# Attention and a gated MLP on one core: the opening loads 288 keys and 512 queries first, and two pairs are turned by DMA

## The chip, the cores and the metric

The kernel runs on one core of one Trainium2 chip. Its time is the device time of one execution in microseconds (us); a lower time is better. A core has five engines with a queue of instructions each: TensorE (PE in the profile; matrix products and transposes), VectorE (DVE), ScalarE (ACT), GpSimd (POOL) and SyncE (SP, which here only issues DMAs). DMAs issued by SP and ACT go through hardware queues (q1 and q10 in the profile), those of GpSimd through a software queue (q0); all are carried out by the same sixteen DMA engines. An engine does its instructions in the order in which they stand in its queue, and an instruction that waits holds up all behind it.

## The reference

Attention for 8 batches of 8 heads (576 positions, head size 64) with a bias that depends on the distance of two positions, then a two-layer network with a periodic activation:

```python
scores = scale * np.matmul(q, k.transpose(0, 1, 3, 2))
bias = bias_table[bucket]                       # bucket of |i - j|
scores = scores + bias.transpose(2, 0, 1)[None, :, :, :]
attn = softmax(scores)
x = (attn @ v).transpose(0, 2, 1, 3).reshape(B * S, H * D)   # 4608 x 512
h = x @ w_in                                    # 512 -> 2048
s = np.sin(alpha * h)
g = h + s * s / (alpha + 1e-09)
out = g @ w_out                                 # 2048 -> 512
```

## The kernel before

Heads are worked on in pairs (64 + 64 rows of the 128 partitions), four pairs (0 to 3) to a batch. For a pair the keys and queries are brought into the form head-size x position (`kT`, `qT`). A **score unit** is one block of 128 keys against 512 queries of both heads of a pair: two matmuls into PSUM, one exponential on ScalarE that writes `u` in half precision, one multiplication on VectorE by the exponential of the bias (`m2r`). A pair has four such units ("A") and one for the last 64 keys ("C"), whose bias tile is `mhr`. Then TensorE forms u times v (AV), with a column of ones that gives the sum; VectorE divides (a reciprocal `rd` and a product, the normalization), and the result, positions x features, is turned into features x positions, `xT`. Products of `xT` with `w_in`, the activation and products with `w_out` follow. Attention of the next batch runs between these.

The first batch is special: nothing covers it. Its keys and queries are loaded in single precision (`natx` for pair 0, on SP's queue, `nat` for pairs 1 to 3, by GpSimd), converted, and transposed on TensorE (lines 594 and 600), 96 positions at a time, then copied out of PSUM (L583). Fillers (`zz`) keep TensorE running meanwhile. The bias table goes a way of its own: `tabN` and `phi_sb` are multiplied on TensorE, exponentiated on ScalarE (`tabE`), multiplied with `phi_sb` again, copied to `e_sb` (L649), written to DRAM in `e_dram` from ScalarE's queue (L650), and read back by SP in the shifted forms `m2r` (L516) and `mhr` (L523). GpSimd's copy `tick` (L675) waits for `m2r`, and the loads of `w_in` (L481) stand behind it. `clear` (L491 to L497) sets the padding of `kt`, `vh` and `v` once for each of two buffers. The normalizations of pairs 0 to 2 (L1056, L1057) give the tile `s`, which TensorE turns with four transposes each (L1088) and VectorE or ScalarE copies into `xT` (L583, L581). Later batches turn theirs with a DMA transpose from SP's queue (L1079, L970).

The order on each engine is made when the program is built: the class `Plan` holds tasks with a cost on each engine that may take them, a priority and for some a due time `nb`, and its `run` plays them through with these costs and writes each engine's instructions in the order that comes out. The constants in capitals (`T_...` due times in us, `..0` priorities of the first batch) set that order and nothing else: on the chip each instruction waits for its inputs, not for a due time. The units of the first batch come in this order:

```python
runs = ((a, "A", 0), (a, "A", 1), (a, "A", 2), (a, "C", 0), (a, "A", 3),
        (b, "A", 0), (b, "A", 1), (b, "C", 0), (b, "A", 2), (b, "A", 3))
```

for the pairs a, b = 0, 1 and then 2, 3.

Of the kernel before, what the change touches and what calls it, by code (L numbers as in the profile page):

```python
# [64 lines left out]
class Plan:  # L65
# [89 lines left out]

    def run(self, t0):
        free = {e: t0 for e in ("PE", "ACT", "DVE", "POOL", "SP")}
        todo = list(self.tasks)
        while todo:
            best = None  # L160
            cands = {e: [] for e in free}
            over = []
            look = 0
            for t in todo:
                look += 1
                if look > WINDOW:
                    break
                r = self.ready(t)
                if r is None:
                    continue  # L170
                for e in t.engs:
                    if e == "ACT" and t.s_only and not self.sin:
                        continue
                    st = max(free[e], r)
                    if t.fill and self.in_qk and self.used >= OFFSET + self.quota * self.share:
                        over.append((st, t))
                        continue
                    cands[e].append((st, t))
            if over and min((x[0] for x in cands["PE"]), default=1e9) > free["PE"] + FILL_GAP * min(
                    x[1].part for x in over):  # L180
                cands["PE"] += over
            for e, c in cands.items():
                if not c:
                    continue
                s0 = min(x[0] for x in c)
                st, t = min(((x[0], x[1]) for x in c if x[0] <= s0 + SLACK[e]),
                            key=lambda x: (x[1].pri, x[0]))
                fin = st + t.engs[e]
                if best is None or (st, fin) < best[:2]:
                    best = (st, fin, e, t)  # L190
            if best is None:
                raise RuntimeError("nothing can go on")
            st, fin, e, t = best
            if e == "PE" and WARM_FROM < free[e] < WARM_END and st > free[e] + WARM_GAP:
                if self.fill(free[e], 192):
# [29 lines left out]
WARM_END = 22.0  # L225
QUOTA = 47
QUOTA1 = 28
OFFSET = 0
T_START = 4.0
STEPS = {0: ((1, 1, 1, 1),) * 3, 1: ((3, 1),) * 3}  # L230
T_W0 = 24.5
PRI_S = 0
T_WI = 16.8
T_TAB = 5.2
T_CL = 24.5
T_FIRST = (4.75, 5.95)
T_PAIR = ((7.9, 8.5), (9.3, 10.2), (11.6, 12.3))
T_ACT = ()
T_M2 = (14.6, 15.4, 16.6, 17.2)
T_MH = 15.4  # L240
T_RST = 25.0
T_V0 = (5.8, 6.4, 8.9, 9.6)
T_P3 = 7.0
T_VA = (10.5, 11.0)
T_VB = 19.5
V_AT = {1: (4, 5, 6, 7)}
V_PRI = -1000
T_AL = (10.0, 560)
LATE = 100
P_ST = 3  # L250
WIDE = 3
T_TP = ((150, 150), (650, 650), (1500, 1500))
GA = 0.0
GB = 0.0
GUARD = {"A": GA, "B": GB, "C": 0.0, "X": 0.0}
T_LD = 33.0

AV_AT = (3, 4, 6, 7)
AV_D = (0, 0, 300, 0)
# [7 lines left out]
MIX = "nnssss"  # L267
SUMS = {1: (0, 1, 2, 3)}
PACE = ((0, 0), (0, 0), (2, 1), (8, 1))
T_WS = (43.0, 48.3, 48.3, 48.3)  # L270
# [9 lines left out]
T_V = ((15.5, 19.0), (50.0, 50.0))  # L280
T_TR1 = ((32.0, 33.5), (35.0, 36.5))
T_W = (25.5, 30.5)
T_WO = (40.5, 43.0, 45.7, 48.3)
WARM0 = 8
WARM1 = 2
WARM_LAG = 0.3
WARM_GAP = 0.12
WARM_FROM = 7.3
AV_PRI = 0
NORM_PRI = 200  # L290
CP_PRI = 0
# [16 lines left out]
def kernel(  # L308
# [39 lines left out]
    for x in range(EW - 1):  # L348
# [39 lines left out]


    natx = tp.tile([128, NF * DM], F16, name="natx", tag="g", bufs=2)  # L390
    N0 = 2 * 2 * SI * D
    nat0 = natx[0:SN, 0 : 2 * N0].bitcast(F32).rearrange("s (kq h x) -> s kq h x", kq=2, h=2)
    natb = natx[0:SN, 2 * N0 : 3 * N0].rearrange(
        "s (kq i two d) -> s kq i two d", kq=2, i=SI, two=2
    )
# [65 lines left out]
    def load_v32(h):  # L461
        nc.sync.dma_start(out=vst[:, h], in_=v[0, h, 0:512].rearrange("(c p) d -> p c d", p=128))
# [10 lines left out]
    def load_nat(dst, h0, h1, src, eng):  # L473

        eng.dma_start(out=dst, in_=src[h0:h1].rearrange("h (p i) d -> p h (i d)", i=SI))
# [30 lines left out]
    def warm1(k, n):  # L506
        full(pb[:, k, 0:n], zz[:, 0:128], zz[:, 0:n], True, True)

    def cast0(kq, eng):
        eng.tensor_copy(  # L510
            out=natb[:, kq], in_=nat0[:, kq].rearrange("s two (i d) -> s i two d", i=SI)
        )

    def load_m2r(eng, h0, h1, r):

        eng.dma_start(  # L516
# [18 lines left out]
    load_nat(nat0[:, 0], 0, 2, k[0], nc.sync)  # L535
    load_nat(nat0[:, 1], 0, 2, q[0], nc.sync)
# [19 lines left out]
    cast0(0, nc.vector)  # L556
    x0 = nat0[:, 1].rearrange("s two (i d) -> s i two d", i=SI)
    nc.vector.tensor_copy(out=natb[:, 1, :, 0], in_=x0[:, :, 0])
    P_.tensor_copy(out=natb[:, 1, :, 1], in_=x0[:, :, 1])

    def loads2():
        for h in (0, H // 2):
# [22 lines left out]
    def plan_tr(t, p, kq, pri, nb, deps=()):  # L585
# [42 lines left out]

        return [x], [plan.add({"POOL": 0.4 if t == 0 else 0.5}, tail, [x], pri + 30)]

    def plan_table():

        a, b = Buf("h"), Buf("h")
# [12 lines left out]
            full(bank(b)[0:H, 0:EW], tabE, phi_sb, True, True)  # L646

        def cp(e):
            nc.scalar.activation(out=e_sb, in_=bank(b)[0:H, 0:EW], func=AF.Copy)  # L649
# [12 lines left out]
        plan.add({"ACT": 1.1}, cp, [x], -1100, use=[b])  # L662

    def plan_v0():
        plan.add({"POOL": 1.4}, lambda e: load_pair(3), [], 9001, nb=T_P3)
# [141 lines left out]
    def plan_att0(g, gates, gate):  # L807

        u, ub, done = Cell(), Buf("u"), {}
        a, b = 2 * g, 2 * g + 1  # L810
        runs = ((a, "A", 0), (a, "A", 1), (a, "A", 2), (a, "C", 0), (a, "A", 3),
                (b, "A", 0), (b, "A", 1), (b, "C", 0), (b, "A", 2), (b, "A", 3))
        exps, head = [], []
        for i, unit in enumerate(runs):
            base = PB + 3200 * g + 300 * i
            x = plan_unit(0, *unit, u, ub, done, gate, base)
            p, kind, _ = unit
            deps = gates + tr[(0, p, 0)][1 if kind == "C" else 0] + tr[(0, p, 1)][0]

            def run(e, i=i, x=x):  # L820
                if i == 0:
# [183 lines left out]
    def plan_av(t, parts, u, ub, done, base, dma):  # L1005
# [65 lines left out]
            rows = S * t + q0, S * t + parts[-1][1] + 128  # L1071
            xdone.append((t, rows, p0, x))

        if dma:

            def turn(e):
                o = (xT[:, p0 : p0 + 2, x0 : x0 + 128] if two else
                     xT[:, p0, x0 : x0 + 128 * nq].rearrange("d (c q) -> d c q", c=nq))
                nc.sync.dma_start_transpose(  # L1079
                    out=o, in_=xn.v[:, 0:nq].rearrange("p c d -> p (c d)"))  # L1080

            made(plan.add({"SP": 0.3}, turn, [x], base, use=[xb]))
            return
# [376 lines left out]
        plan.sin = name == SIN_SET  # L1460

    PB = 0
    tr = {(0, 0, kq): plan_tr(0, 0, kq, -1000, T_FIRST[kq]) for kq in range(2)}
    vdone, lds, spans = [], [], {}
    plan_table()
    plan_v0()
# [94 lines left out]
```

## Time and profile before

| | before |
|---|---|
| median of 3 timed runs | 364.24 us (363.93 to 364.65) |
| span of the profiled execution (first to last instruction) | 361.6 us |
| TensorE busy | 356.0 us, 98% of the span |
| ScalarE busy | 316.3 us, 87% |
| VectorE busy | 306.1 us, 85% |
| GpSimd busy | 93.2 us, 26% |
| first score, first exponential | 8.02 us, 8.45 us |
| from where TensorE has no gap any more | 28.97 us |

The profile is of one execution, whose own time is given as its span alone; the timed runs lie 2.6 us above it. Times in it count from the start of the span. A row of the timeline has start, length, engine, line, operation, output <- input, and in brackets how long the engine had been idle before it and what ended that. In the list of a window's DMAs the last number is the median time from issue to landing.

### The profile page before, as it was taken

Reading aid. Unit: us, or ns where it says so; the run is one execution under the profiler, and the core shown is the slowest. Engines: PE = TensorE matmul, PEld = TensorE weight load, DVE = VectorE, ACT = ScalarE, POOL = GpSimd, SP = SyncE. Lnnn points to the kernel's source line nnn. Section 1 sums busy time; section 2 is a strip of 40 time slices with the busy share of each in tenths; the row PEclk is TensorE's granted clock in tenths of the full one; section 3 lists DMA queues with packets and bytes.
Section 4 is the critical chain, followed back from the end, with each engine's and each line's share of the span. In section 5 each row is a group of like instructions: output and inputs, shape, how many; then the busy total and the mean of one; then the engine's idle time right before and its main releaser. Section 6 shows DMA issues by size and latency. Waiting matters only on the chain.

```text
span 361.6 us, 9613 instructions
## 1 busy us (share of the span) xinstructions
PE 356.0 (98%) x3811; PEld 218.4 (60%) x3811; DVE 306.1 (85%) x749; ACT 316.3 (87%) x436; POOL 93.2 (26%) x135
## 2 busy tenths in 40 slices
PE   8999999999999999999999999999999999999996
PEld 4564445644575447884684458545787467456685
DVE  4887888989977998699978997899869986999982
ACT  2998999999998999899989999899989998996811
POOL 8577450064000820055001900091006000000000
PEclk9999999999999999999999999999999999999999
DMA  9999999789724994299918992699339322001023
GB/s 167 206 200 188 207 160 134 142 83 124 120 48 104 138 150 101 55 158 143 137 34 159 110 169 55 127 136 143 87 81 158 66 57 54 15 3 59 31 76 101
DMA packets 150157, 40.53 MB, mean 112 GB/s; under 512 B 137224, under 2 KB 145504, under 8 KB 150112
## 3 DMA queue, kind: packets, MB, share of 16 engines
q0 software_dynamic: 96064, 17.67, 60.7%
q1 hardware_dynamic: 53872, 22.16, 26.1%
q8 instruction: 30, 0.49, 0.6%
q10 hardware_dynamic: 176, 0.09, 0.1%
q14 instruction: 15, 0.12, 0.1%
HBM read 37.73 MB, written 16.56 MB: 150 GB/s over the span
## 4 chain that ended last, share of the span: by engine, by line
PE 94%; DMA 2%; ACT 1%; DVE 1%; SPq 0%; issue 0%; DVEq 0%
PE pb L500 93%; DMA mhr<-e_dram 1%; ACT u L749 1%; DMA e_dram<-e_sb 1%; PE pb L600 1%; PE pb L1088 1%; DVE u L780 1%; DVE s L1057 0%; SPq L523 0%; ACT e_sb L649 0%; PE pb L594 0%; ACT xT L581 0%; SPq L516 0%; DVE outs L1314 0%; DVE zz L551 0%
## 5 line engine op out<-in xcount | busy, mean ns | idle before, releaser
L749 ACT ACTIVATE u<-pb 128x1024 f16<-128x1024 f32 (+1 forms) x146 | 136.8, 1020 | 6.2 <-PE pb L500 4.9
L500 PE MATMUL pb<-xT,w_in 128*128 128x512 f16 (+4 forms) x704 | 128.6, 340 | 0.3 <-ACT xT L581 0.3
L1146 DVE SCALAR_TENSOR_TENSOR g<-sq,inv_a,pb 128x512 f16<-128x512 f16 x144 | 101.4, 744 | 3.8 <-ACT sq L1139 1.8
L1132 ACT ACTIVATE s<-pb,alphaT 128x512 f16<-128x512 f32 x144 | 92.9, 693 | 12.4 <-PE pb L500 11.6
L500 PEld LDWEIGHTS <-w_in 128*128 128x128 f16 x704 | 64.5, 98 | 56.0 <-issue 0.8
L500 PE MATMUL pb<-w_out,g 128*128 128x512 f16 (+1 forms) x416 | 83.5, 339 | 0.0
L500 PEld LDWEIGHTS <-g 128*128 128x128 f16 x552 | 50.8, 98 | 34.8 <-issue 5.2
L780 DVE TENSOR_TENSOR u<-u,m2r 128x512 f16<-128x512 f16 (+1 forms) x128 | 61.5, 488 | 9.9 <-ACT u L749 9.2
L500 PEld LDWEIGHTS <-u 128*128 128x128 f16 x1280 | 55.9, 97 | 9.6 <-issue 4.9
L1139 ACT ACTIVATE sq<-s 128x512 f16<-128x512 f16 x76 | 47.5, 640 | 2.0 <-DVE g L1146 1.1
L445 POOL COPY kt<-kT 64x256 f16<-64x256 f16 x12 | 5.2, 430 | 168.0 <-DMA kT<-staged_k 167.7
L500 PE MATMUL pb<-v,u 128*128 128x65 f16 x1024 | 43.8, 193 | 0.0
L500 PE MATMUL pb<-qT,kT 64*128 64x64 f16 (+1 forms) x512 | 42.1, 285 | 0.8 <-DVE qT L583 0.3
L1141 DVE TENSOR_TENSOR sq<-s 128x512 f16<-128x512 f16 x68 | 28.4, 427 | 11.3 <-ACT s L1132 10.4
L500 PEld LDWEIGHTS <-kT 64*128 64x128 f16 x512 | 17.2, 94 | 20.5 <-issue 13.1
L500 PE MATMUL pb<-vh,u 128*128 128x130 f16 x128 | 28.3, 221 | 0.2 <-DVE s L1057 0.2
L1000 DVE TENSOR_TENSOR xn<-pb,rd 128x384 f16<-128x384 f32 (+2 forms) x53 | 26.0, 490 | 1.8
L450 POOL DMA_DIRECT2D v<-in_v_dram x28 | 24.7, 895 | 3.1 <-DMA nat<-in_k_dram 1.8
L1459 ACT ACT_TABLE_LOAD x15 | 19.2, 1283 | 0.3
L749 ACT ACTIVATE nat<-pb 128x1024 f16<-128x1024 f32 (+1 forms) x24 | 18.8, 820 | 0.0
L999 DVE RECIPROCAL rd<-pb 128x6 f32<-128x6 f32 (+2 forms) x53 | 9.9, 187 | 8.2 <-PE pb L500 7.0
L500 PE MATMUL pb<-wsum,g 128*128 128x256 f16 (+1 forms) x136 | 16.7, 267 | 0.0
(100 smaller groups left out, 311.7 us busy)
## 6 DMA issues: line engine op xcount, KB each, us to landing
out_dram<-outs SPq DMA_DIRECT2D x28, 256.0 KB, 3.0
v<-in_v_dram POOLq DMA_DIRECT2D x28, 128.0 KB, 4.8
staged_k<-in_k_dram POOLq DMA_DIRECT2D x6, 576.0 KB, 8.6
staged_q<-in_q_dram POOLq DMA_DIRECT2D x6, 576.0 KB, 12.1
w_in<-in_moe_w_in_dram POOLq DMA_DIRECT2D x4, 512.0 KB, 9.1
w_out<-in_moe_w_out_dram POOLq DMA_DIRECT2D x4, 512.0 KB, 13.5
out_dram<-outs SPq DMA_DIRECT2D x16, 128.0 KB, 1.7
w_out<-in_v_dram SPq DMA_DIRECT2D x6, 128.0 KB, 5.1
```

The source lines that it names most:

```text
L445: nc.gpsimd.tensor_copy(out=kts[t % 2][r, :, r], in_=kTs[t % 2][r, :, 512:S])
L450: nc.gpsimd.dma_start(out=vs[t % 2][:, c, :, 0:D], in_=vp[128 * c : 128 * c + 128],)
L500: nc.tensor.matmul(out=out, lhsT=lhsT, rhs=rhs, start=start, stop=stop, skip_group_check=go_on)
L749: nc.scalar.activation(out=o, in_=x, func=AF.Exp, scale=0.125)
L780: nc.vector.tensor_tensor(out=io, in0=io, in1=m2[:, 2 * p : 2 * p + 2, x0 : x0 + hi - lo], op=ALU.mult)
L999: nc.vector.reciprocal(out=r, in_=x[:, :, :, D])
L1000: nc.vector.tensor_tensor(out=xn[:, 0:n].rearrange("p c (z d) -> p c z d", z=2), in0=x[:, :, :, 0:D], in1=r.unsqueeze(3).to_broadcast([128 ...
L1132: nc.scalar.activation(out=s16.v, in_=h.v, func=AF.Sin, scale=alphaT[:, f : f + 1])
L1139: nc.scalar.activation(out=sq.v, in_=s16.v, func=AF.Square)
L1141: k_of(e).tensor_tensor(out=sq.v, in0=s16.v, in1=s16.v, op=ALU.mult)
L1146: nc.vector.scalar_tensor_tensor(out=gcell[b].v[:, f, :], in0=sq.v, scalar=inv_a[:, f : f + 1], in1=h.v, op0=ALU.mult, op1=ALU.add,)
L1459: nc.scalar.preload_act_table_set(name)
```

## The change

It rebuilds the first 30 us and leaves the later batches as they are.

- Pair 0's keys and queries come in four loads: 288 keys (96 rows of three), 512 queries (128 rows of four), the other 288 keys (72 rows of four), and the last 64 queries. The conversion of the 512 queries and the copy of their transposes are halved over ScalarE and VectorE; the other keys are converted by GpSimd; the tail copies of pair 0's keys (`kt`) move from GpSimd to VectorE.
- GpSimd's loads begin later: the seven clears of the first buffer move from VectorE to GpSimd, ahead of the loads of pairs 1 and 2, and pair 3's loads get a later due time.
- The write of `e_dram` and the load of `alphaN` move from ScalarE's queue to SP's, and `phi_sb` is loaded ahead of `tabN`.
- The xT of pairs 0 and 1 of the first batch are turned by a DMA transpose of 128 x 4 x 128 each from SP's queue (`DT0 = 2`) instead of by TensorE and a copy.
- The warm-up has one filler of 512 and one of 192 less, and nearly all due times become about 1.5 us earlier. The normalizations of pairs 0 to 2 get a lower priority (`NORM0` 900 to 1500), their AV products a higher one.

```diff
-T_START = 4.0
+T_START = 3.4
...
+DT0 = 2
...
+RUN0 = "aaaca aacaa"
+U0 = 400
...
-T_P3 = 7.0
+T_P3 = 9
...
-T_AL = (10.0, 560)
+T_AL = (10.0, 2160)
...
-AV0 = 1500
+AV0 = 500
...
-NORM0 = 900
+NORM0 = 1500
...
-WARM0 = 8
-WARM1 = 2
+WARM0 = 7
+WARM1 = 1
...
+    for x_, rows_, n_ in (("k0", SK, 3), ("q", 128, NQ), ("k1", SR, 4), ("qt", 64, 1)):
...
+    load_first("k0", k, 0, K0, nc.sync)
+    load_first("q", q, 0, 512, nc.sync)
+    nc.scalar.dma_start(out=phi_x, in_=phi_h.ap())
     nc.scalar.dma_start(out=tabN, in_=bias_table)
-    nc.scalar.dma_start(out=phi_x, in_=phi_h.ap())
-    nc.scalar.dma_start(out=alphaN, in_=moe_alpha.rearrange("(f p) -> f p", p=128))
+    load_first("k1", k, K0, S, nc.sync)
+    nc.sync.dma_start(out=alphaN, in_=moe_alpha.rearrange("(f p) -> f p", p=128))
     load_v32(0)
     load_v32(1)
+    load_first("qt", q, 512, S, nc.sync)
...
+    nc.vector.memset(zz, 0.0)
+    clear(P_, 0)
     load_pair(1)
     load_pair(2)
     P_.tensor_copy(out=idf_sb, in_=id_sb[0:NF, 0:NF])
-    nc.vector.memset(zz, 0.0)
-    clear(nc.vector, 0)
...
+        k0 = one("k0", 3, kTs[0][:, 0, 0:K0], T_LAND[0], C_K0, Y_K0, P_K0)
+        qs = one("q", NQ, qTs[0][:, 0, 0:512], T_LAND[1], C_Q, Y_Q, P_Q)
+        k1 = one("k1", 4, kTs[0][:, 0, K0:S], T_LAND[2], C_K1, Y_K1, P_K1)
+        qt = one("qt", 1, qTs[0][:, 0, 512:S], T_LAND[3], (("DVE", 1, 0.13),), (("DVE", 1),), P_QT)
...
-            nc.scalar.dma_start(
+            nc.sync.dma_start(
                 out=e_dram.ap()[:, 0:H].rearrange("r h x -> h r x"),
...
-        if dma:
+        if dma or wide and p0 < DT0:
 
             def turn(e):
+                if wide:
+                    nc.sync.dma_start_transpose(
+                        out=xT[:, p0, x0 : x0 + 512].rearrange("d (c q) -> d c q", c=4),
+                        in_=xn.v.rearrange("p c d -> p (c d)"))
+                    return
```

In `plan_first`, which is new, `one` makes the conversions, transposes and copies of one of the four parts: `casts` and `copies` name the engine and how many of the part's columns it takes (`C_Q` and `Y_Q` are `(("ACT", 2, ...), ("DVE", 2, ...))`).

The order on the engines at three places. First GpSimd's queue up to the loads of pair 3, which are the last two `nat_96` rows (`natx` is pair 0, `vh` and `v` the values). Before:

```order
12 L475 DMA nat_96<-in_q_dram 96x2x384
13 L550 CAST idf_sb<-id_sb 16x16
14 L559 CAST natx<-natx 96x6x64
15 L469 DMA vh_74<-in_v_dram 64x4x64
16 L625 COPY kt_70<-kT_66 64x64 x2
17 L469 DMA vh_74<-in_v_dram 64x4x64
18 L475 DMA nat_96<-in_k_dram 96x2x384
19 L475 DMA nat_96<-in_q_dram 96x2x384
```

Of the change:

```order
15 L522 MEMSET v_72 128x32
16 L500 DMA nat_96<-in_k_dram 96x2x384
...
19 L500 DMA nat_96<-in_q_dram 96x2x384
20 L577 CAST idf_sb<-id_sb 16x16
21 L604 CAST natx<-natx 72x512
22 L494 DMA vh_74<-in_v_dram 64x4x64 x2
23 L490 CAST v_72<-w_out_79 128x4x64
24 L500 DMA nat_96<-in_k_dram 96x2x384
25 L500 DMA nat_96<-in_q_dram 96x2x384
26 L646 COPY kt_70<-kT_66 64x64 x2
```

The clears, of which row 15 is the last, now stand ahead of all loads; a pair of tail copies moved behind pair 3's loads, and a conversion of values ahead of them.

Second VectorE's queue from the multiplication by `mhr` (the C unit of pair 0) to the normalization of pair 0. Before:

```order
24 L766 TENSOR_TENSOR u<-u,mhr 128x128
25 L780 TENSOR_TENSOR u<-u,m2r 128x2x256 x2
26 L780 TENSOR_TENSOR u<-u,m2r 128x2x384 x2
27 L780 TENSOR_TENSOR u<-u,m2r 128x2x256
28 L1056 RECIPROCAL rd<-pb 128x8
29 L1057 TENSOR_TENSOR s_375<-pb,rd 128x512
```

Of the change:

```order
16 L846 TENSOR_TENSOR u<-u,mhr 128x128
17 L860 TENSOR_TENSOR u<-u,m2r 128x2x256 x2
18 L771 COPY alphaT<-pb 128x16
19 L772 TENSOR_SCALAR tmp_a<-alphaT 128x16
20 L775 RECIPROCAL inv_a<-tmp_a 128x16
21 L604 COPY qT_68<-pb 128x576
22 L860 TENSOR_TENSOR u<-u,m2r 128x2x384
23 L604 COPY qT_68<-pb 128x64
24 L860 TENSOR_TENSOR u<-u,m2r 128x2x384
25 L860 TENSOR_TENSOR u<-u,m2r 128x2x256 x2
26 L860 TENSOR_TENSOR u<-u,m2r 128x2x384
27 L1140 RECIPROCAL rd<-pb 128x8
```

The alpha rows, the copy of pair 3's queries and that of the last 64 queries of pair 0, which stood far ahead of the first multiplication or did not exist, now stand between, and two multiplications more.

Third TensorE's queue where pair 3's AV products begin (`vh_74`, the values of the last 64 keys), and SP's at the transposes that TensorE's first products with `w_in` read. Before:

```order
554 L500 MATMUL pb<-v_72,u 128x65
555 L500 LDWEIGHTS w_in_78
556 L500 MATMUL pb<-xT,w_in_78 128x512
...
562 L500 MATMUL pb<-xT,w_in_78 128x512
563 L500 LDWEIGHTS u
564 L500 MATMUL pb<-vh_74,u 128x130
```

Of the change:

```order
528 L525 MATMUL pb<-v_72,u 128x65
529 L525 LDWEIGHTS w_in_78
530 L525 MATMUL pb<-xT,w_in_78 128x512
531 L525 LDWEIGHTS w_in_78
532 L525 MATMUL pb<-xT,w_in_78 128x512
533 L525 LDWEIGHTS u
534 L525 MATMUL pb<-vh_74,u 128x130
```

And SP of the change, where the rows of `s` are pairs 0 and 1:

```order
11 L536 DMA m2r<-e_dram 128x4x384
12 L487 DMA w_out_79<-in_v_dram 128x4x64 x4
13 L1162 DMA_TRANSPOSE xT<-s_386 128x4x128
14 L1162 DMA_TRANSPOSE xT<-s_443 128x4x128
15 L1295 DMA out_dram<-outs 128x512 x2
```

Two products instead of four stand ahead of pair 3's AV, in the same place, and what they read comes from SP's first transpose.

More of the change, by code (lines that the diff above doesn't have):

```diff
@@ L629, in plan_tr, with plan_first, cast, turn @@
         return [x], [plan.add({"POOL": 0.4 if t == 0 else 0.5}, tail, [x], pri + 30)]
+    def plan_first():
+        def cast(o, i, engs, nb, pri):
+            return plan.add(engs, lambda e: copy_on(e, o, i), [], pri, nb=nb)
+        def turn(parts, rows, dst, deps, pri, copies):
+            b, c = Buf("mo"), Cell()
+            n = len(parts)
+            def mm(e):
+                c.v = bank(b).bitcast(F16)
+                for i, x in enumerate(parts):
+                    nc.tensor.transpose(
+                        out=c.v[:, rows * i : rows * i + rows], in_=x, identity=id_sb[0:rows, 0:rows]
+                    )
+            m = plan.add({"PE": 0.02 + n * T_TURN * rows / 96}, mm, deps, pri, new=[b])
+            made = []
+            for e, a, z in copies:
+                def cp(e, a=a, z=z):
+                    copy_on(e, dst.rearrange("d (p i) -> d p i", i=n)[:, :, a:z],
+                            c.v[:, 0 : n * rows].rearrange("d (i p) -> d p i", i=n)[:, :, a:z])
+                w = (z - a) * rows
+                made.append(plan.add({"DVE": 0.07 + w / 830.0} if e == "DVE" else {"ACT": 0.07 + w / 1150.0},
+                                     cp, [m], pri, use=[b]))
+            return m, made
+        def one(x_, n, dst, nb, casts, copies, pris):
+            f, o = first[x_]
+            x = f.rearrange("s two (i d) -> s i two d", i=n)
+            a, cs = 0, []
+            for e, w, d in casts:
+                cs.append(cast(o[:, a : a + w], x[:, a : a + w], {e: d}, nb, pris[0]))
+                a += w
+            b, cp = 0, []
+            for e, w in copies:
+                cp.append((e, b, b + w))
+                b += w
+            m, z = turn([o[:, i] for i in range(n)], x.shape[0], dst, cs, pris[1], cp)
+            m.pad = ((192,) * PAD_FIRST,)
+            return z
+        k0 = one("k0", 3, kTs[0][:, 0, 0:K0], T_LAND[0], C_K0, Y_K0, P_K0)
+        qs = one("q", NQ, qTs[0][:, 0, 0:512], T_LAND[1], C_Q, Y_Q, P_Q)
+        k1 = one("k1", 4, kTs[0][:, 0, K0:S], T_LAND[2], C_K1, Y_K1, P_K1)
+        qt = one("qt", 1, qTs[0][:, 0, 512:S], T_LAND[3], (("DVE", 1, 0.13),), (("DVE", 1),), P_QT)
+        def tail(e):
+            for z in range(2):
+                r = slice(64 * z, 64 * z + 64)
+                k_of(e).tensor_copy(out=kts[0][r, 0, r], in_=kTs[0][r, 0, 512:S])
+        tl = plan.add({"DVE": 0.3}, tail, k1, T_TL)
+        tr[(0, 0, 0)] = k0 + k1, [tl]
+        tr[(0, 0, 1)] = qs, qs
+        tr["first"] = k0 + qs
@@ L810, in plan_att0 @@
         a, b = 2 * g, 2 * g + 1
-        runs = ((a, "A", 0), (a, "A", 1), (a, "A", 2), (a, "C", 0), (a, "A", 3),
-                (b, "A", 0), (b, "A", 1), (b, "C", 0), (b, "A", 2), (b, "A", 3))
+        runs = []
+        for p, kinds in zip((a, b), RUN0.split()):
+            n = iter(range(4))
+            runs += [(p, "C", 0) if x == "c" else (p, "A", next(n)) for x in kinds]
         exps, head = [], []
         for i, unit in enumerate(runs):
-            base = PB + 3200 * g + 300 * i
+            base = PB + 3200 * g + U0 * i
             x = plan_unit(0, *unit, u, ub, done, gate, base)
@@ L1462 @@
     PB = 0
[L1463 removed]
+    tr = {}
+    plan_first()
     vdone, lds, spans = [], [], {}
```

97 lines of the change are left out of this document (56 added, 41 removed).

## The prediction

> **What bounds the kernel now.** I read the totals first, then the windows, to see where TensorE is not full.
>
> ```profile
> span 361.6 us, 9613 instructions
> PE 356.0 (98%) x3811; PEld 218.4 (60%) x3811; DVE 306.1 (85%) x749; ACT 316.3 (87%) x436; POOL 93.2 (26%) x135
> 29.00:60.00 31.00, 31.00 (x320) 14.83 (x321) 26.51 (x64) 29.58 (x44) 14.26 (x21) 1.00 1.67 184
> 60.00:358.60 298.60, 298.49 (x3161) 187.90 (x3159) 259.11 (x636) 265.22 (x366) 57.26 (x64) 1.00 0.78 97
> ```
>
> The first number behind a window's length is TensorE's busy time: 31.00 of 31.00 us, then 298.49 of 298.60. From 29 us on there is no gap, and the clock column says 1.00. So a change in the opening is worth exactly what it moves the start of that unbroken stretch, plus work that it takes out of the stretch. The median of the three timed runs, 364.24 us, is 2.6 us above the span; I carry that unchanged. Next I followed the chain of waits through the opening (start, length, what).
>
> ```profile
> 6.85 0.60 ACT e_sb L649
> 7.46 2.94 DMA e_dram<-e_sb
> 11.63 4.59 DMA mhr<-e_dram
> 16.34 0.23 DVE u L766
> 18.89 0.70 DVE s L1057
> 28.97 5.99 PE pb L500 x27
> ```
>
> This says that the start at 28.97 hangs on the bias table: its write (e_dram), its load (mhr, landed 16.22), VectorE's multiplications by it, then pair 0's normalization (L1057). The first keys and queries are not on it. An earlier first score pays only so far as this chain moves too.
>
> **The change, part by part.** *The first scores.* The timeline (start, length, engine, line) of before:
>
> ```profile
> 3.92 0.64 DVE L510 CAST natx<-natx 96x768 f16<-96x768 f32 x1 [1.15 <-DMA natx<-in_k_dram]
> 5.32 0.35 DVE L558 CAST natx<-natx 96x384 f16<-96x384 f32 x1 [0.76 <-DMA natx<-in_q_dram]
> 5.35 0.69 POOL L559 CAST natx<-natx 96x384 f16<-96x384 f32 x1 [0.74 <-DMA natx<-in_q_dram]
> 7.21 0.76 DVE L583 COPY qT<-pb 128x576 f16<-128x576 f16 x1 [0.75 <-PE pb L594]
> 8.02 0.39 PE L500 MATMUL pb<-qT,kT 64*128 64x512 f16 x2 [0.27 <-DVE qT L583]
> 8.45 1.02 ACT L749 ACTIVATE u<-pb 128x1024 f16<-128x1024 f32 x1 [1.01 <-PE pb L500]
> ```
>
> The casts of the queries were released by their load, at 5.32, and the first score came 2.70 later. GpSimd's half of the cast took 0.69 and goes to ScalarE; VectorE's equal half took 0.35, so 0.34 is saved if ScalarE does as well. The copy of 0.76 is split over two engines: 0.36 saved. The keys that stand in front of the queries are half as many bytes and GpSimd's own loads start 1.9 us later, so I let the queries land 0.7 earlier (bounds 0 and 1.4, the lead that the keys' cast at 3.92 has in the rows). Sum: 1.4 us, first exponential near 7.05; the two fewer fillers of the warm-up fit inside that. The second half of the keys is needed only by the second score and has the time of one exponential, 0.9 us, as cover. The alpha load moved to SP's queue and the swapped table loads cost nothing: both are wanted later than they land.
>
> *GpSimd later.* The seven clears run between these rows of the next batch's own clears, 1.95 us, and pair 3's load was issued at 7.71 and landed 3.9 later:
>
> ```profile
> 24.45 0.31 POOL L491 MEMSET kt<- 64x256 f16 x1
> 26.15 0.25 POOL L497 MEMSET v<- 128x32 f16 x1
> 7.71 0.65 POOL L475 DMA_DIRECT2D nat<-in_k_dram  x1
> nat<-in_k_dram POOLq DMA_DIRECT2D x1, 144.0 KB, 3.9
> 12.73 0.39 PE L500 MATMUL pb<-qT,kT 64*128 64x512 f16 x2
> 13.27 0.45 PE L600 MATMUL pb<-id_sb,nat 96*64 96x96 f16 x12
> 11.95 2.88 ACT L749 ACTIVATE u<-pb 128x1024 f16<-128x1024 f32 x3
> ```
>
> Of the 1.95, GpSimd's old wait for the queries (0.74, in the row of L559) absorbs a part; one pair of tail copies moves behind the load and a cast ahead of it, which I set off against each other: the load is issued at 7.71 + 1.95 - 0.74 = 8.9 and lands at 12.8. TensorE's stream has pair 3's key transposes ahead of pair 1's second score (at 12.73 in before); they found their load landed at 11.6, now they wait for it. Transposes (0.45) and a score's lead over its exponential (0.43, from 8.02 to 8.45) put that exponential at 13.7 plus their handovers, about 13.9; in before it ran second in the row that starts at 11.95, with 0.9 from one to the next, plus one more: 13.75. So the 1.4 us of the head are gone at the seventh exponential.
>
> *The bias table.* Its copy is reached some 0.5 us earlier, its write now goes through SP's queue, where only loads that need it stand behind. But pair 3's and the values' loads now lie where the table is read back. Bounds for the landing: 0.5 earlier, 1.0 later; I take no shift.
>
> *VectorE up to the first normalization.*
>
> ```profile
> 10.53 0.17 DVE L691 COPY alphaT<-pb 128x16 f32<-128x16 f32 x1
> 10.95 0.25 DVE L695 RECIPROCAL inv_a<-tmp_a 128x16 f32<-128x16 f32 x1
> 13.76 0.76 DVE L583 COPY qT<-pb 128x576 f16<-128x576 f16 x1 [0.37 <-PE pb L600]
> 16.48 2.26 DVE L780 TENSOR_TENSOR u<-u,m2r 128x512 f16<-128x512 f16 x5
> 18.66 0.20 DVE L1056 RECIPROCAL rd<-pb 128x8 f32<-128x8 f32 x1
> 18.89 0.69 DVE L1057 TENSOR_TENSOR s<-pb,rd 128x512 f16<-128x512 f32 x1
> ```
>
> Between the mhr product and the normalization stood five multiplications (2.26). Now there are seven (two more at 0.45: 0.9), the alpha trio (10.53 to 11.20: 0.67), pair 3's query copy (0.7 with overlap) and a 64-wide copy (0.1, an estimate from the 0.76 for 576). They were done ahead of the table's landing, in idle time; now they stand behind it. That is 2.3, of which I take 2.2: the normalization ends at 21.8 instead of 19.6.
>
> *Two pairs turned by DMA.* Eight transposes of TensorE and two copies of VectorE go. They lie ahead of the unbroken stretch and save nothing at its end. In their place SP issues a DMA transpose at 21.8, and TensorE's next products with w_in wait for it, in order, ahead of pair 3's AV products. What else runs at that time, and what such a transpose took beside traffic and without it:
>
> ```profile
> q0 software_dynamic: 864, 1.67, 111.7%
> xT<-xn SPq DMA_TRANSPOSE x1, 2.3
> 168.45 2.44 SPq L970 DMA_TRANSPOSE xT<-xn  x2
> q0 software_dynamic: 5422, 0.69, 246.0%
> xT<-xn SPq DMA_TRANSPOSE x2, 5.7
> DMA to landing us min/median/max: 2.3/2.8/6.7
> ```
>
> The first row is the queue of GpSimd's loads over 20 to 28 us: it has all sixteen DMA engines, and no packet of another data queue runs. Alone a transpose takes 2.3. The two issued at 168.45, under GpSimd's staging loads, took 5.7: from 168.0 to 172.4 only that queue's 5422 packets ran, so theirs came in the last stretch. The longest of all took 6.7. The case at 21.8 is nearest to these two, so I take 6.2 (bounds 2.3 and far above 6.7, since the loads here have larger packets and this transpose is larger): pair 0 is turned at 28.0.
>
> ```profile
> 24.82 1.02 PE L500 MATMUL pb<-xT,w_in 128*128 128x512 f16 x4
> 25.68 0.22 PE L500 MATMUL pb<-vh,u 128*128 128x130 f16 x1
> 27.12 0.38 PE L500 MATMUL pb<-xT,w_in 128*128 128x512 f16 x1
> ```
>
> Four products went in 0.86, so the two that stand there now take 0.43: pair 3's AV begins at 28.43 instead of 25.68, 2.75 later. One product that stood ahead of 28.97 now comes behind: 0.22. The next product with w_in stood 1.44 behind (27.12) and needs pair 1, normalized two or three multiplications and 0.9 later, about 23.9, so turned at 30.1; TensorE is there at 29.87: 0.23 more. Sum: 2.75 + 0.22 + 0.23 = 3.2, and 364.24 + 3.2 = **367.4 us**. From 5.6 to 6.7 for the turning, and half a microsecond either way for the normalization, that case spans 366.3 to 368.4.
>
> **The rivals.** *The opening as it is meant, faster.* The table lands 1.4 earlier with everything else, VectorE's additions vanish in its waits, and the turning takes its 2.3. Then the stretch begins up to 1.4 earlier: 362.8, up to 363.6 where the table gives less. For it: nothing but the table's landing held VectorE at 16.34, and a lone transpose is short. Against: pair 3's late load, and that chain. *The turning in time, the gain eaten.* At 2.3 to 3.5 pair 0 is turned by 25.3, where TensorE comes by, and only the late pair 3 and the table decide: 364.0 to 365.1. For it this row, of SP's queue from 17.0 to 19.5 us, with w_in's loads issued since 17.1:
>
> ```profile
> 17.12 2.92 POOL L481 DMA_DIRECT2D w_in<-in_moe_w_in_dram  x4
> q1 hardware_dynamic: 1757, 0.46, 90.7%
> ```
>
> There SP's queue ran on beside w_in; but w_in's stream was only starting. *Turn by turn, slower still.* The transpose is served one packet, then one of w_in's. In 20 to 28 us 864 packets ran, each engine one in 0.15 us; a transpose of 128 KB in the 256-byte packets in which this kernel's others move has 32 for each engine, which adds 4.7 to the 2.3 and more for each further packet of w_in let through: 7 to 12 us, an end at 368.4 to 374. It decides once the turning takes over 6.7.
>
> The Trainium skill, page "DMA: Bandwidth & Descriptors", section "Queues, rings and completion order", says that each DMA engine goes round-robin over the queue rows that have work, a packet at a time. By that the transposes at 168.45 should have got turns at once; the row of 168.0 to 172.4 shows none, so the trace does not bear it out there.
>
> **How the numbers follow.** Turning as in the loaded rows: 0.42. Turn by turn: 0.16. In time, gain eaten: 0.20. As meant: 0.22. About 0.2% (0.7 us) is what a measurement of this kernel can tell from no change. Faster by more than that, under 363.5, is nearly all of "as meant" with little of "eaten": 0.22. Within 0.2%: 0.15. Slower: the two slow cases and the upper end of "eaten": 0.63. The range 363.0 to 370.0 leaves out the lowest part of "as meant" (0.05) and the long half of "turn by turn" (0.1).
>
> **What would show it.** Right: TensorE idle for over 2 us near 25 to 28 ahead of w_in products, released by the DMA of xT; that DMA's landing time over 5 us; pair 0's normalization at 21 to 22; the unbroken stretch from 32. The head: first score near 6.6. Wrong: xT landing within 4 us, or the mhr load landing before 15.5 and the normalization below 20.

## The result: 9.2 us slower, and the profile after

| | before | changed |
|---|---|---|
| median of 4 timed runs each | 364.44 us | 373.60 us (373.11 to 375.30) |
| ratio, 95% interval | | 1.0258 (1.0229 to 1.0288) |
| span of the profiled execution | 361.6 us | 371.3 us |
| first score, first exponential | 8.02, 8.45 us | 6.72, 7.15 us |
| pair 0 normalized | 19.58 us | 24.70 us |
| pair 3's AV begins | 25.68 us | 33.95 us |

The forecast was 367.4 with a range of 363.0 to 370.0: right in sign, far too small. From the page and the windows (length, then busy time of TensorE with its instructions, its weight loads, VectorE, ScalarE, GpSimd; then TensorE's granted clock, the DMA share and GB/s) of the changed kernel:

```profile
span 371.3 us, 9600 instructions
PE 356.1 (96%) x3798; PEld 219.0 (59%) x3798; DVE 305.7 (82%) x744; ACT 317.8 (86%) x439; POOL 94.5 (25%) x140
17.00:26.00 9.00, 5.57 (x85) 4.21 (x85) 8.31 (x19) 5.89 (x7) 5.26 (x11) 0.81 1.08 212
19.00:21.00 2.00, 1.78 (x17) 1.15 (x16) 1.97 (x7) 1.51 (x2) 2.00 (x4) 0.50 1.03 174
29.00:35.00 6.00, 1.86 (x19) 1.34 (x20) 0.77 (x2) 1.08 (x1) 5.87 (x12) 0.79 1.24 179
33.00:35.00 2.00, 1.86 (x19) 1.34 (x20) 0.00 (x0) 0.00 (x0) 2.00 (x4) 0.50 1.30 199
60.00:368.00 308.00, 307.92 (x3265) 192.56 (x3263) 265.72 (x655) 274.24 (x376) 58.05 (x64) 1.00 0.81 98
```

TensorE does the same 356 us of work and is full from 60 us on; nearly all of the loss is ahead of that. It stands in two places, 17 to 26 and 29 to 35 us, and behind each the clock column shows 0.50, half speed, for 2 us at least (19 to 21 and 33 to 35; the longer windows average over it). The timeline of the changed kernel shows both stands, with what ended them in brackets:

```profile
5.83 0.38 ACT L602 ACTIVATE qT<-pb 128x256 f16<-128x256 f16 x1 [0.59 <-PE pb L664]
6.24 0.42 DVE L604 COPY qT<-pb 128x256 f16<-128x256 f16 x1 [0.91 <-ACT qT L602]
6.72 0.39 PE L525 MATMUL pb<-qT,kT 64*128 64x512 f16 x2
15.70 1.36 DVE L860 TENSOR_TENSOR u<-u,m2r 128x512 f16<-128x512 f16 x3 [2.30 <-DMA m2r<-e_dram]
18.19 0.43 DVE L860 TENSOR_TENSOR u<-u,m2r 128x512 f16<-128x512 f16 x1 [0.42 <-DMA m2r<-e_dram]
18.53 0.17 DVE L771 COPY alphaT<-pb 128x16 f32<-128x16 f32 x1
18.75 0.19 PE L664 MATMUL pb<-id_sb,natx 64*128 64x64 f16 x1 [2.53 <-DVE alphaT L771]
20.24 0.32 PE L525 MATMUL pb<-vh,u 128*128 128x130 f16 x1
20.49 3.37 DVE L860 TENSOR_TENSOR u<-u,m2r 128x768 f16<-128x768 f16 x4
22.47 0.82 PE L525 MATMUL pb<-qT,kT 64*128 64x512 f16 x6
22.90 2.86 ACT L829 ACTIVATE u<-pb 128x1024 f16<-128x1024 f32 x3 [2.04 <-PE pb L525]
24.01 0.69 DVE L1141 TENSOR_TENSOR s<-pb,rd 128x512 f16<-128x512 f32 x1
24.73 3.60 SPq L1162 DMA_TRANSPOSE xT<-s  x2
33.14 1.01 PE L525 MATMUL pb<-xT,w_in 128*128 128x512 f16 x2 [4.66 <-DMA xT<-s]
33.95 0.32 PE L525 MATMUL pb<-vh,u 128*128 128x130 f16 x1
37.58 0.38 ACT L602 ACTIVATE xT<-pb 128x256 f16<-128x256 f16 x1 [0.38 <-PE pb L1177]
53.62 1.02 PE L525 MATMUL pb<-w_out,g 128*128 128x512 f16 x4 [0.38 <-DMA vh<-in_v_dram]
```

Read downwards: the first score comes 1.30 earlier. Then VectorE waits for the table's loads, 2.30 for the first part of `m2r` (15.70) and 0.42 for the second (18.19), and behind these waits stands a small copy, `alphaT`. TensorE needs the place in PSUM which that copy frees and stands for 2.53 us; after that it runs at half clock. Pair 0's AV products, which stand next, take 2.23 us (20.24 to 22.47). In the kernel before they took 1.30, from the first of these rows to the second:

```profile
16.81 0.22 PE L500 MATMUL pb<-vh,u 128*128 128x130 f16 x1
18.11 0.39 PE L500 MATMUL pb<-qT,kT 64*128 64x512 f16 x2
```

The next scores stand behind these products, so ScalarE has none for 2.04 us, VectorE's last four multiplications ahead of the normalization take 3.37 us with their waits, and the normalization is late. Then pair 0's DMA transpose, issued at 24.73 and landed 8.27 us later at 33.00, keeps TensorE for another 4.66 us.

The sum: pair 3's AV begins 8.27 later than before (33.95 against 25.68; that the transpose took 8.27 too is chance). From there to the last copy of xT it takes 3.63 where it took 2.86 (28.54 - 25.68), at the lower clock: 0.77. That makes 9.04. One w_in product moved behind that place (0.22), but the gap of 0.26 that the kernel before had at 28.97 is gone, and the two cancel: the last key transposes of the next batch start 9.06 later (51.57 against 42.51). A last wait comes at 53.62: 0.38. The last instruction of all starts 9.32 later (367.95 against 358.63); the other 0.38 of the 9.7 between the spans lies behind it, where only the output is still being written.

### The profile page after: what moved, and what is told of

Its sections match the earlier page's. It is cut to its first block, busy times and chain, and to the rows that moved or that the text cites. A ratio compares the mean times of both kernels' runs of the same rounds, so it can differ in the third digit from the quotient of the medians.

```text
span 371.3 us, 9600 instructions
## 1 busy us (share of the span) xinstructions
PE 356.1 (96%) x3798; PEld 219.0 (59%) x3798; DVE 305.7 (82%) x744; ACT 317.8 (86%) x439; POOL 94.5 (25%) x140
## 3 DMA queue, kind: packets, MB, share of 16 engines
q1 hardware_dynamic: 55404, 22.47, 26.1%
## 4 chain that ended last, share of the span: by engine, by line
PE 86%; DMA 8%; DVE 2%; POOL 1%; issue 0%; SPq 0%; ACT 0%; DVEq 0%
PE pb L525 86%; DMA vh<-in_v_dram 3%; DMA w_out<-in_moe_w_out_dram 3%; DMA m2r<-e_dram 1%; DVE u L860 1%; DMA e_dram<-e_sb 1%; POOL nat L500 1%; PE pb L1177 0%; SPq L543 0%; POOL u L846 0%; DVE s L1141 0%; ACT u L829 0%; ACT e_sb L602 0%; PE pb L664 0%; DVE tmp_a L772 0%
## 5 line engine op out<-in xcount | busy, mean ns | idle before, releaser
L860 DVE TENSOR_TENSOR u<-u,m2r 128x512 f16<-128x512 f16 (+1 forms) x128 | 63.1, 499 | 11.7 <-ACT u L829 8.4
L525 PEld LDWEIGHTS <-u 128*128 128x128 f16 x1280 | 57.5, 99 | 12.2 <-issue 7.7
L525 PE MATMUL pb<-v,u 128*128 128x65 f16 x1024 | 45.0, 196 | 0.0
L458 POOL DMA_DIRECT2D staged_q<-in_q_dram x6 | 16.7, 2786 | 0.0
```

Source lines behind the costliest of these rows:

```text
L458: nc.gpsimd.dma_start(out=dst.ap()[t].rearrange("s (h d) -> s h d", h=H), in_=src[t].rearrange("h s d -> s h d"),)
L525: nc.tensor.matmul(out=out, lhsT=lhsT, rhs=rhs, start=start, stop=stop, skip_group_check=go_on)
L860: nc.vector.tensor_tensor(out=io, in0=io, in1=m2[:, 2 * p : 2 * p + 2, x0 : x0 + hi - lo], op=ALU.mult)
```

## The experiments

Each ran beside the kernel before on the same chip; ratios are to it. The chip is not the same for all.

**e1_pe_turn**: the changed kernel, TensorE turns the pairs.

```diff
-DT0 = 2
+DT0 = 0
```

> The changed kernel with one constant back (DT0 = 0): TensorE turns pairs 0 and 1 again. Theory A (the wait for the DMA transpose, 4.7 us at 28.5 in the changed kernel, is one of two losses; the other is that pair 0's normalization ends at 24.7 instead of 19.6): the wait goes, AV of pair 3 starts near 29.2 instead of 33.9, time 368 to 369, still 3.5 to 4.5 above the kernel before. Theory B (the DMA transpose is the whole loss): 363 to 365.

Measured: 367.78 us, ratio 1.0081 (1.0054 to 1.0108). The DMA turns are 5.8 of the 9.2 us by these medians; the rest is another loss, as theory A had it. Its profile, of an execution of 370.19 us, has the stand at the same instruction. It is longer there, and m2r's second load landed at 19.31 instead of 18.09:

```profile
19.96 0.21 PE L664 MATMUL pb<-id_sb,natx 64*128 64x64 f16 x1 [3.54 <-DVE alphaT L771]
```

**e2_alpha_early**: the changed kernel with `T_AL = (10.0, 560)`.

> The changed kernel with the alpha transposes and VectorE's three alpha instructions early again (T_AL priority 560), the DMA turns kept. Theory A (TensorE's 2.5 us stand at 18.75 is for the PSUM bank that alphaT's late copy frees, and it delays the scores and the normalization): the stand goes, normalization ends near 22.5 to 23, the DMA transposes are issued some 2 earlier. If their length from issue holds (8.3), they land near 31 and the time is 371 to 371.5. Theory B (they wait for the backlog of w_in's loads to empty, whenever they are issued): they still land near 32 to 33, time 372.5 to 373.5.

Measured: 373.73 us, ratio 1.0251 (1.0211 to 1.0292): no gain, theory B. Timeline of e2 and its transpose from issue to landing; then the DMA engines of the changed kernel from 28.5 to 31.5 us and from 31.5 to 32.5 us (queue: packets, MB, share of 16 engines):

```profile
23.13 0.69 DVE L1141 TENSOR_TENSOR s<-pb,rd 128x512 f16<-128x512 f32 x1
33.53 1.01 PE L525 MATMUL pb<-xT,w_in 128*128 128x512 f16 x2 [5.94 <-DMA xT<-s]
xT<-s SPq DMA_TRANSPOSE x1, 9.6
q0 software_dynamic: 222, 0.44, 94.0%
q1 hardware_dynamic: 218, 0.06, 17.9%
q1 hardware_dynamic: 691, 0.17, 122.1%
q0 software_dynamic: 20, 0.02, 9.3%
```

Normalized 0.9 earlier, pair 0 is turned 0.4 later than in the changed kernel: the transpose took 9.6 instead of 8.3. What is won ahead of it is lost in it, as long as w_in's loads run. The windows show this for the changed kernel: nothing of the transpose runs before 28.5, 218 packets (out of 512 for each pair) go in the 3 us in which w_in's stream (q0) still runs, and 691 in the one us after it has run dry. Pair 0 lands at 33.0 and w_in's last load at 32.5; in e2 at 33.4 and 33.1.

**e3_turn_alone**: the kernel before, with only the two pairs turned by DMA.

```diff
-        if dma:
+        if dma or wide and p0 < 2:
             def turn(e):
+                if wide:
+                    nc.sync.dma_start_transpose(out=xT[...], in_=xn.v...)
+                    return
```

> The kernel before with one part of the change alone: pairs 0 and 1 turned by DMA. Its normalization ended at 19.6, just when the stream of w_in's loads fills the DMA engines. Theory A (8.3 from issue under that stream): pair 0 lands near 28, TensorE stands 3 us there, time 368 to 370. Theory B (landing tied to the end of w_in's backlog, 31.1): stand of 6, time 370.5 to 372. The step of the prediction (6.2): lands at 25.8 to 26, about 366.

Measured: 375.70 us, ratio 1.0304 (1.0268 to 1.0339), worse than all parts together and than any of the three forecasts. Timeline, landing, and two windows of the DMA engines (20.3 to 24 us, then 27 to 30 us):

```profile
31.79 0.59 PE L500 MATMUL pb<-xT,w_in 128*128 128x512 f16 x1 [6.56 <-DMA xT<-s]
35.41 2.29 PE L500 MATMUL pb<-xT,w_in 128*128 128x512 f16 x5 [3.04 <-DMA xT<-s]
xT<-s SPq DMA_TRANSPOSE x1, 11.3
q0 software_dynamic: 378, 0.74, 110.6%
q1 hardware_dynamic: 7, 0.00, 0.2%
q0 software_dynamic: 278, 0.54, 94.2%
q1 hardware_dynamic: 279, 0.07, 17.6%
```

For 3.7 us after the issue the transpose gets nothing (378 packets of GpSimd's queue, on which w_in comes; the 7 of the other queue ran in the first 0.1 us). Later it is turn by turn: 278 packets of w_in and 279 of the transpose in the same 3 us. One of w_in's has 2 KB, one of the transpose's 256 bytes, so at 93 a us pair 0's 512 packets take 5.5 us, an estimate from this window. Here, unlike in the changed kernel, they are through before w_in's stream ends (pair 0 landed at 31.65, w_in's last load at 32.76). The Trainium skill, page "DMA: Bandwidth & Descriptors", section "Queues, rings and completion order", says that an engine goes round the queue rows that have work, packet by packet. The 278 to 279 agree with it if a packet of the profile is one of the page's, which the profile does not tell; the first 3.7 us do not show it.

**e4_clears_first**: the kernel before, with only the clears moved to GpSimd ahead of its loads.

```diff
+    clear(P_, 0)
     load_pair(1)
     load_pair(2)
...
-    clear(nc.vector, 0)
```

> The kernel before with one part alone: the seven clears on GpSimd ahead of its loads. Theory A (later loads of GpSimd fall together with the reading back of the bias table and make the second m2r load land 1.4 later, 18.1 instead of 16.7): time 365.3 to 366. Theory B (the table is late for another reason, the write from SP's queue): the load still lands near 16.7, time 364 to 364.8.

Measured: 364.38 us, ratio 0.9997 (0.9982 to 1.0013). The m2r load in question landed at 17.03 instead of 16.73; the clears alone are not what makes the table late.

**e5_half_packets**: e3 with w_in in eight loads of 512 columns.

> The kernel before with the DMA turns alone, as in e3_turn_alone, but w_in loaded by eight DMAs of 512 columns instead of four of 1024, so that its packets have 1024 bytes instead of 2048. Theory A (after a first wait of 3.7 us the DMA engines take one transpose packet for each packet of w_in; 512 packets of pair 0 over 16 engines are 32 turns of 0.17 to 0.2 us): the turns take half as long, pair 0's transpose lands some 8 us after its issue instead of 11.4, and the time falls by about 3 us to 372 to 373. Theory B (it gets a share of the bytes, or waits for the backlog): still 11 us, time 375 to 376.

Measured: 376.44 us (two runs), ratio 1.0335 (1.0290 to 1.0380), no gain: theory A fell as stated. The DMA windows show why (28 to 30 us, then 26.5 to 28 us):

```profile
q0 software_dynamic: 298, 0.29, 86.3%
q1 hardware_dynamic: 291, 0.07, 29.3%
q0 software_dynamic: 79, 0.08, 48.4%
q1 hardware_dynamic: 35, 0.01, 23.1%
xT<-s SPq DMA_TRANSPOSE x1, 11.7
```

Turn by turn holds, and a turn is shorter as expected: 146 transpose packets a us instead of 93. But from 19.98, its issue, to 25 us no packet of it ran, and soon after its first ones all traffic fell to a third of its bytes for 1.5 us. The start and this hole cost more than the turns give back. What sets them is open; e3 has such a hole too, from 26.0 to 26.5 (12 packets in all).

**e9_stream_later**: e3 with w_in's loads behind GpSimd's casts (`T_WI = 21.5`).

> As e3_turn_alone, but GpSimd issues w_in's four loads behind its casts of the values, near 22.8 instead of 17.9 to 20.1, so that pair 0's transpose, issued near 20.3, meets no stream. Theory A (the stream of w_in's packets is what makes the transpose long): it lands in 2.3 to 3, near 23, TensorE's wait at that place turns into one for w_in itself (first piece near 28), time 367 to 370. Theory B (the transpose is long at this place for a reason of its own, such as its source in the normalization or the size): it still takes 8 to 11.

Measured: 370.21 us (two runs), ratio 1.0153 (1.0128 to 1.0178). The transpose, issued at 20.59, took 4.3 instead of 11.3. Nothing of it ran before 21.8; the row of queue q1 is from 21.8 to 23 us. TensorE's stand there is for w_in's late load:

```profile
xT<-s SPq DMA_TRANSPOSE x1, 4.3
q1 hardware_dynamic: 541, 0.13, 54.6%
29.33 1.04 PE L500 MATMUL pb<-xT,w_in 128*128 128x512 f16 x4 [3.81 <-DMA w_in<-in_moe_w_in_dram]
```

So it is mainly the stream that makes the transpose long, not its place or its size: theory A, though 4.3 is more than the 2.3 to 3 expected of it. Without the stream the first packet still takes some 1.3 us, so of the 3.7 us of e3 about 2.4 or more are the stream's, and all packets go through in 1.2 us instead of 5.5. The loads that delayed it cannot be moved away for nothing; they are needed at 25 us.

**e6_pe_turn_alpha**: the changed kernel with `DT0 = 0` and the alpha instructions early.

> The changed kernel with TensorE turning the pairs and the alpha instructions early. Theory A (with the turning gone, the 3.5 us stand of TensorE at alphaT's bank, seen in e1_pe_turn, is on the path): the stand goes, pair 0's normalization ends near 23.5 instead of 25.9, time 365.5 to 366.5. Theory B (the multiplications wait for m2r's second load anyway, and the stand is covered): 367.3 to 368.3, as e1_pe_turn.

Measured: 367.98 us, ratio 1.0092 (1.0068 to 1.0117), no gain over e1. The stand for `alphaT` is gone, and another took its place:

```profile
18.57 0.75 DVE L604 COPY qT<-pb 128x576 f16<-128x576 f16 x1
19.37 0.37 PE L525 MATMUL pb<-zz 128*128 128x256 f16 x1 [2.04 <-DVE qT L604]
```

The copy of pair 3's queries stands behind the same multiplications. So it was not the alpha copy as such: both copies did this that TensorE needs and that the order puts behind VectorE's wait for the table.

**e7_write_from_act**: e6, with the table written from ScalarE's queue.

```diff
-            nc.sync.dma_start(
+            nc.scalar.dma_start(
                 out=e_dram.ap()[:, 0:H]...
```

> As e6_pe_turn_alpha, and e_dram is written from ScalarE's queue again. Theory A (the write takes 4.2 us behind the value loads on SP's queue, 2.9 on its own): the write takes under 3.2, m2r's second load lands a us earlier, time a us below e6_pe_turn_alpha. Theory B (the queue makes no difference; the loads of values and pair 3 that run at that time do): the same as e6_pe_turn_alpha within 0.5.

Measured: 367.25 us, ratio 1.0080 (1.0052 to 1.0108), which cannot be told from e6. In the profiles m2r's second load landed at 18.37, against 18.13 in e6, not a us earlier: theory B.

**e10_due_times**: e6, with the table's due times as before.

```diff
-T_M2 = (13.2, 13.8, 15.2, 15.8)
-T_MH = 14.0
-T_WI = 15.6
+T_M2 = (14.6, 15.4, 16.6, 17.2)
+T_MH = 15.4
+T_WI = 16.8
```

> As e6_pe_turn_alpha, with three due times of the bias table (T_M2, T_MH, T_WI) put back to those of before, some 1.4 later; on the chip they only move instructions: VectorE's copy of pair 3's queries goes ahead of all multiplications. Theory A (with the due times too early, copies that TensorE needs stand behind multiplications that wait for the table, and TensorE stood 2.0 at 19.4 in e6_pe_turn_alpha): that stand goes, normalization of pair 0 ends near 22, time 365 to 366. Theory B (the table's late landing, 18.1, decides alone): as e6_pe_turn_alpha, 367 to 368.

Measured: 365.13 us, ratio 1.0040 (1.0012 to 1.0068): theory A. Up to pair 0's normalization VectorE's order differs from that of e6 in one place: the query copy is ahead of the multiplications. Pair 0 is normalized 1.5 earlier than in e6 (23.72):

```profile
14.06 0.76 DVE L604 COPY qT<-pb 128x576 f16<-128x576 f16 x1 [0.16 <-PE pb L621]
16.22 1.36 DVE L860 TENSOR_TENSOR u<-u,m2r 128x512 f16<-128x512 f16 x3 [1.40 <-DMA m2r<-e_dram]
19.32 2.11 DVE L860 TENSOR_TENSOR u<-u,m2r 128x768 f16<-128x768 f16 x4
21.58 0.69 DVE L1141 TENSOR_TENSOR s<-pb,rd 128x512 f16<-128x512 f32 x1
```

The four multiplications that took 3.37 us in the changed kernel take 2.11. TensorE's long stand is gone, and with it the half clock: 1.00 in this execution, 0.62 from 17 to 26 us in e6's (shown at the end). So the gain is that of both; they were not told apart.

**e12_loads_early**: e10, with the second keys converted by VectorE and pair 3's and the values' loads early.

```diff
-C_K1 = (('POOL', 4, 0.65),)
-T_P3 = 9
-T_V0 = (5.5, 6.0, 10.1, 8.8)
+C_K1 = (('DVE', 4, 0.45),)
+T_P3 = 5
+T_V0 = (4.6, 4.6, 5.1, 5.1)
```

> As e10_due_times, with the second half of pair 0's keys converted by VectorE instead of GpSimd, and GpSimd's loads of pair 3 and of the values issued as early as its queue allows (near 6 to 9 instead of 8 to 12). Theory A (the table's second m2r load lands at 18.0 instead of 16.7 to 17.6 because these loads run beside it): it lands at or under 17, pair 0's normalization ends near 21, time 363.3 to 364.3. Theory B (the loads' order does not matter, the four-part load itself makes the table late): it still lands near 18, time 365 as e10_due_times.

Measured: 365.93 us, ratio 1.0029 (1.0000 to 1.0059); the kernel before had 364.89 on that chip. The load landed at 17.59 instead of 18.03: some of what theory A said, not enough to be seen in the time. In three kernels whose opening is that of before up to this load (e3, e9, e5) it landed at 17.64, 17.40 and 17.32, and in e4 at 17.03, so 16.73 was an early one.

**e8_head_alone, e11_head_in_order, e13_head_early**: three tries at the head alone: TensorE turns the pairs, the alpha instructions are early, the priorities `NORM0` and `AV0` are those of before and `U0` is 300, the clears are on VectorE and the table is written from ScalarE's queue; e11 with the due times of e10, `T_P3 = 7` and earlier values' loads, e13 with e12's loads.

> The changed kernel with only the four-part load, the halved casts and copies and the earlier due times left: TensorE turns all pairs, clears on VectorE, e_dram from ScalarE's queue, alpha early, and the priorities of normalizations, AV and score units as before. Theory A (the first exponential is 1.3 earlier, but the path goes through the bias table, which is at best 0.5 earlier): 363.8 to 365. Theory B (the intended gain comes through once the rest is undone): 362.5 to 363.3.

> The four-part load with the halved casts and copies alone, and the order around it as in before: e8_head_alone with the due times of the bias table, of pair 3's and of the values' loads put back, so that pair 3's loads go out early and no copy stands behind the table's multiplications. Theory A (the way through the bias table sets the start; the earlier first score gives nothing): 364 to 365.5. Theory B (the 1.3 us at the first exponential come through once the order is right): 362.5 to 363.3.

> As e11_head_in_order (clears on VectorE, so that GpSimd's first loads go out at 1.5), with the same two edits as e12_loads_early: pair 3's and the values' loads near 4.5 to 8. Theory A: the table's second m2r load lands at or under 17 instead of 18.5, w_in follows it and is issued a us earlier, the 2.2 us stand of TensorE for the next batch's keys at 33.9 goes, time 363 to 364.5. Theory B: more early traffic delays pair 0's own queries and the table's write, time 365 or more.

Measured: 370.04, 369.84 and 370.13 us, ratios 1.0165 (1.0127 to 1.0204), 1.0151 (1.0126 to 1.0177) and 1.0148 (1.0088 to 1.0208). That is against both theories of e8 and of e11, and with theory B of e13 in its number, whose reason was not seen. The 370.13 is the middle of three executions of e13 (369.23 to 372.3); a fourth took 2,022 us, and with it the profile, which is of that one, is left out. The timelines of e8 and e11:

```profile
16.65 0.69 PE L621 MATMUL pb<-id_sb,nat 96*64 96x96 f16 x12 [3.98 <-DMA nat<-in_k_dram]
33.91 0.45 PE L621 MATMUL pb<-id_sb,nat 96*64 96x96 f16 x12 [2.23 <-DMA nat<-in_k_dram]
```

In e8 the order put pair 3's load so late that TensorE stood 3.98 us for it. In e11 that is mended, and TensorE reaches the next batch's key transposes after 9 products with w_in, where before did 36 first, and waits 2.23 for their load. These two kernels measure an unfortunate order, not the head. What the rest of their loss is was not told apart, so no run here measures the head alone.

No kernel here beat the one before.

## Why the prediction was wrong, step by step

- **The first scores**: right in number, 6.72 and 7.15 us against 6.6 and 7.05, in part by luck. The queries landed 1.0 earlier (cast from 4.30 instead of 5.32), where I took 0.7. The halved copy saved nothing where I took 0.36: VectorE's half waited for ScalarE's (0.91 in its row), and the two together run from 5.83 to 6.66. That an earlier first score buys nothing by itself fits e10, where the DMA turns and the two misplaced copies are out of the way and 0.9 us at the first exponential (7.55 against 8.45) go with a ratio of 1.0040; other parts of the change are still in e10, so it is not shown.
- **Pair 3's load**: close. Issued at 8.04 and landed at 12.12 (forecast 8.9 and 12.8). No later step failed by it.
- **The bias table**: I took no shift, within 0.5 earlier and 1.0 later. m2r's second load landed at 18.09, 1.4 later than the 16.73 of the profile before, and VectorE's multiplications began at 15.70 instead of 14.43. Part of that was the profile's luck (17.0 to 17.6 in e3, e4, e5, e9); e4 and e7 excuse the clears and the write's queue, and e12 gives some of it to the order of GpSimd's loads. The rest is open.
- **VectorE up to the first normalization**: the step that failed first. I added up what stood in between (two more multiplications, the alpha trio, two copies: 2.2) and had 21.8; it was 24.70. Of the 2.9 us that it was later, some 1.3 are the table's, as just told, and some 1.3 are waits inside the last four multiplications (3.37 against 2.11 in e10). What I did not ask of the moved copies was who waits for them. TensorE waits for their places in PSUM, and the last of the multiplications wait for scores that TensorE then cannot give. So the same row counts twice, once as VectorE's time and once as a stand of TensorE's (2.53), and the half clock behind the stand stretches it. e6 shows it by the copy that took over, e10 by removing it: 2.9 us by the medians.
- **The DMA turns**: right that TensorE would wait for a transpose slowed by w_in's stream, mis-sized. I took 6.2 from the loaded rows; it was 8.27, and 11.3 in e3. My rows were the wrong neighbours: those of 168 us are line 970, a quarter of this transpose (128 x 2 x 64 against 128 x 4 x 128), beside packets of 128 bytes instead of 2 KB. I had noted both differences and priced neither. The rival "turn by turn" had the mechanism that e3 shows, and its 368.4 to 374 holds the result; 0.16 was too little. That its number fits the changed kernel is half luck: there the turns were cut short by the end of w_in's stream (218 packets in 3 us, then 691 in one), and a first wait that no forecast had made up for it. I held the row of 17.0 to 19.5 against this rival, where SP's queue ran on beside w_in, but there SP's loads were queued first. e3 shows the reverse order: the transpose, queued second, waited nearly 4 us for its first packet.
- **The path behind**: pair 3's AV did begin right behind the two products that wait for pair 0, but it began 5.52 later than forecast (33.95 against 28.43). That is 2.90 from the normalization, 2.07 from the transpose, and 0.5 because landing to AV took 0.95 instead of 0.43, at half clock. The 0.22 for the product that moved was made up by a gap of 0.26 that went. Pair 1's transpose cost nothing more (0.23 was reckoned). Not foreseen: the half clock after the stands, 0.77 behind pair 3's AV and 0.9 in pair 0's AV products, and the last wait, 0.38.

By the medians, of the 9.2 us the DMA turns are 5.8 (373.60 to 367.78), the copies behind the table's multiplications 2.9 (367.98 to 365.13, between e6 and e10), and 0.6 is left. These medians come from several chips. By the ratios, each to the kernel before on its own chip, the three are some 6.4, 1.9 and 1.5 us (1.0258 to 1.0081, 1.0092 to 1.0040, and the 1.0040 that stays); the intervals of e6 and e10 just touch. What makes up the part that stays was not found.

## What to carry to other kernels

When an instruction is moved behind a wait on its engine, look first for who needs its output or the buffer that it frees; its own duration is the smaller part. A short DMA on a hardware queue that started under a stream of GpSimd's loads first waited some us here and then got one packet for each of the stream's until the stream ended. So price it by a first wait and its count of packets times the time of the stream's packets, at most to the end of the stream, and take its cost from a row of the same size. Look whether a head start lies on the path that the rest waits for, here the table and the normalization; these runs found no gain in one that does not, though none measured it alone.

## What the runs showed of the hardware

- The DMA engines served a hardware queue and GpSimd's queue one packet each once both were under way (279 to 278 in 3 us beside 2 KB packets, 291 to 298 in 2 us beside 1 KB packets). Before its first packet the transpose, queued second, waited 3.7 to 5 us in e3, e5 and the changed kernel, and 1.3 us in e9, where no stream ran. What it waits for is open.
- In or after most stands of TensorE of 2 us and more its granted clock fell to 0.50 for some us, as in the windows of the changed kernel and in e3 from 28 to 38 us. In e6 it fell with a stand of 2.04 us, as the mean of the window below shows; in e11 the clock stayed at 1.00 after a stand of 2.23, so the length of the stand alone does not decide.

```profile
17.00:26.00 9.00, 6.51 (x87) 5.03 (x86) 7.56 (x16) 5.08 (x6) 5.71 (x11) 0.62 1.06 194
```
